# Two h tiles ahead of the second half of x, and the first w_in cast on one engine, in the first batch of an attention and MLP kernel

## Chip, core, metric

One core of one Trainium2 chip. The metric is device time in microseconds (us) per execution. Kernels that are compared ran in the same rounds on the same chip.

## The reference

Linear attention over 8 batches of 8 heads, 576 positions of 64 dimensions, then an MLP with an exact Gelu, in fp32:

```python
q_s = softmax(q, axis=-1)                 # per position
k_s = softmax(k, axis=2)                  # over positions
kv  = einsum('bhsd,bhse->bhde', k_s, v)
x   = einsum('bhsd,bhde->bhse', q_s, kv)  # -> [4608, 512]
h   = x @ w_in                            # w_in [512, 2048]
g   = 0.5 * h * (1 + erf(h / sqrt(2)))
out = g @ w_out                           # w_out [2048, 512]
```

(The softmaxes are written out in the reference; they are shortened here.)

## The kernel before

Matmuls run in bf16. Heads go in four pairs (hp 0 to 3): pairs 0 and 1 are "half 0", 2 and 3 "half 1". For each batch TensorE does kv, then x from normalised kv (kvc) and transposed q (qT); x is copied from PSUM, the memory into which TensorE writes, to xT in SBUF, from which it reads, one copy per pair; and h tile t (128 of the 2048 columns of h) sums over four dm, the blocks of 128 columns of x, where dm reads xT of pair dm:

```python
    def h_mm(c, ps, t, dms):
        for dm in dms:
            nc.tensor.matmul(
                ps, wi_bf[:, dm, t * 128:(t + 1) * 128], st[c]["xT"][:, dm, :],
                start=(dm == 0), stop=(dm == NDM - 1),
            )
```

In the traces each engine takes its instructions in the order of the program. Batch 0 is the one with little else to do: weights are still arriving. Its part, in the old order:

```python
    kv_mm(0, 0)
    kv_norm(0, 0)                # kvc of half 0: reciprocal and multiply, once per pair
    tp_mm(0, 1)
    tp_evac(0, 1)
    x_tile(0, 2, psum_a, "a")
    x_mm(0, 0)
    x_evac(0, 0, "s")            # "s": ScalarE; else VectorE
    cast_wi_dm(0, wi[0], 0, nc.scalar)
    for dm in range(1, NDM):
        cast_wi_dm(0, wi[0], dm, nc.gpsimd)
    kv_mm(0, 1)
    kv_norm(0, 1)                # kvc of half 1: both pairs at once
    x_evac(0, 1)
    x_tile(0, 3, psum_h, "h")
    x_mm(0, 1)
    x_evac(0, 2, "s")
    x_evac(0, 3)
    cast_wi(1, wi[1], "p")       # second w_in piece (tiles 2, 3), GpSimd
    table(AF.Gelu)
    ...
    h_phase(0, {0: [lambda: cast_wi(2, wi[2], "v")], ...}, groups={0: 2, 4: 4, 8: 4}, ...)
```

`wi[0]` is the first w_in piece, columns 0 to 255, that is h tiles 0 and 1; it is loaded in one transfer and cast to bf16 by dm.

The softmax here doesn't subtract the row's maximum and nothing guards it: scores larger than these inputs give would overflow.

Of the kernel before, what the change touches and what calls it, by code (L numbers as in the profile page):

```python
# [8 lines left out]
FP32 = mybir.dt.float32  # L9
# [7 lines left out]
def kernel(  # L17
# [16 lines left out]
    nc = tc.nc  # L34
# [4 lines left out]
    M = 128 * J  # L39
    R = S - M  # L40
    HP = H // 2
    NDM = DM // 128
# [10 lines left out]
    psum_h = ctx.enter_context(tc.tile_pool(name="psum_h", bufs=3, space=bass.MemoryType.PSUM))  # L53
    psum_y = ctx.enter_context(tc.tile_pool(name="psum_y", bufs=2, space=bass.MemoryType.PSUM))
    psum_a = ctx.enter_context(tc.tile_pool(name="psum_a", bufs=1, space=bass.MemoryType.PSUM))
# [12 lines left out]
    kvc = [singles.tile([128, HP, D], BF16, name=f"kvc{b}") for b in range(B)]  # L68
# [9 lines left out]
    def table(func):  # L78
        nc.scalar.activation(out=scr[:, 1:2], in_=scr[:, 0:1], func=func)  # L79

    st = [dict() for _ in range(B + 1)]
# [83 lines left out]
        for hp in range(HP):  # L165
            cast_v(b, hp)

    def kv_tiles(b):


        if b == 0:
            p = [psum_h.tile([128, 512], FP32, tag="h", name="kv")[:, 0:256] for i in range(2)]
            ps = psum_a.tile([128, 4, 256], FP32, tag="a2", name="kv")
            st[b]["kvall"] = ps[:, 0::2]
            p += [ps[:, 0, :], ps[:, 2, :]]
        else:
            ps = psum_a.tile([128, 4, 256], FP32, tag="a2", name="kv")
            st[b]["kvall"] = ps
            p = [ps[:, i, :] for i in place]
        st[b]["kv"] = p  # L180

    place = [1, 2, 0, 3]

# [4 lines left out]
    def kv_mm(b, half):  # L188


        if "kv" not in st[b]:
            kv_tiles(b)
        for n in range(NS):
            for i in range(2):
                for hh in range(2):
                    hp = 2 * half + i
                    pr = slice(hh * 64, hh * 64 + 64)
                    c = slice((hh ^ i) * 64, (hh ^ i) * 64 + 64)
                    nc.tensor.matmul(  # L199
                        st[b]["kv"][hp][c, 0:D + 1], ek[b % 2][pr, hp, n, :],  # L200
                        v_aug[b % 2][pr, hp, n, 0:D + 1], start=(n == 0), stop=(n == NS - 1),
                    )

    def kv_norm(b, half=None):

        ps = st[b]["kvall"]
        if half is None:
            parts = [(ps, kvc[b], 4)]
        elif b == 0 and half == 0:
            parts = [(st[b]["kv"][hp].unsqueeze(1), kvc[b][:, hp:hp + 1], 1) for hp in range(2)]  # L210
        elif b == 0:
            parts = [(ps, kvc[b][:, 2:4], 2)]
        else:
            parts = [(ps[:, 1:3] if half == 0 else ps[:, 0::3], kvc[b][:, 2 * half:2 * half + 2], 2)]
        for src, dst, m in parts:
            rec = small.tile([128, 4], FP32, tag="reck")
            nc.vector.reciprocal(rec[:, 0:m], src[:, :, D])
            nc.vector.tensor_tensor(  # L218
                out=dst, in0=src[:, :, 0:D],
                in1=rec[:, 0:m].unsqueeze(2).to_broadcast([128, m, D]), op=ALU.mult,  # L220
            )
# [39 lines left out]
    def tp_evac(b, half, eng="v"):  # L261
        o = st[b]["qT"][:, :, 2 * half:2 * half + 2, :]
        if eng == "v":
            nc.vector.tensor_copy(out=o, in_=st[b][f"tp{half}"])
        else:
            nc.scalar.copy(out=o, in_=st[b][f"tp{half}"])
# [12 lines left out]
    def x_tile(b, hp, pool, tag):  # L279
        if "xT" not in st[b]:  # L280
            st[b]["xT"] = attn_sb.tile([128, HP, M], BF16, tag="xT", name="xT")
        st[b][f"x{hp}"] = pool.tile([128, M], FP32, tag=tag, name="ps")

    def x_mm(b, half):

        for bb in range(B if b == B else 1):
            for r in range(2):
                for i in range(2):
                    hp = 2 * half + i
                    pr = slice(r * 64, r * 64 + 64)  # L290
                    c = slice((r ^ i) * 64, (r ^ i) * 64 + 64)
                    ps = st[b][f"x{hp}"]
                    if b < B:
                        nc.tensor.matmul(  # L294
                            ps[c, :], kvc_of(b, hp)[pr], st[b]["qT"][pr, :, hp, :],
                            start=True, stop=True,
                        )
                    else:
                        nc.tensor.matmul(  # L299
                            ps[c, bb * R:(bb + 1) * R], kvc_of(bb, hp)[pr],  # L300
                            st[b]["qT"][pr, bb // 2, hp, bb % 2 * R:(bb % 2 + 1) * R],
                            start=True, stop=True,
                        )

    def x_all(b):

        for hp in range(HP):
            pool, tag = (psum_h, "h") if hp < 3 else (psum_a, "a")
            x_tile(b, hp, pool, tag)
        x_mm(b, 0)  # L310
        x_mm(b, 1)
        for hp, eng in ((0, "s"), (2, "v"), (1, "s"), (3, "v")):
            x_evac(b, hp, eng)

    def x_evac(b, hp, eng="v"):
        ps = st[b][f"x{hp}"]
        if eng == "v":
            nc.vector.tensor_copy(out=st[b]["xT"][:, hp, :], in_=ps)  # L318
        else:
            nc.scalar.copy(out=st[b]["xT"][:, hp, :], in_=ps)  # L320

    def h_begin(c):
        st[c]["g"] = moe_sb.tile([128, NDF, M], BF16, tag="g", name="g", bufs=1)
# [8 lines that stand above are left out]
    def h_gelu(c, ps, t):  # L332
        nc.scalar.activation(out=st[c]["g"][:, t, :], in_=ps, func=AF.Gelu)  # L333
# [75 lines left out]
    def load_wi(i):  # L409

        w = wst.tile([128, NDM, 512], FP32, tag="w")
        n = wi_cols[i]
        src = moe_w_in[:, wi_off[i]:wi_off[i] + n].rearrange("(c p) f -> p c f", p=128)
        d = NDM // wi_parts[i]
        for c in range(0, NDM, d):
            nc.sync.dma_start(out=w[:, c:c + d, 0:n], in_=src[:, c:c + d])
        return w
# [3 lines left out]
    def cast_wi(i, w, eng):  # L421
        n = wi_cols[i]
        r = n // 128
        o = wi_bf[:, :, wi_off[i]:wi_off[i] + n].rearrange("p d (c m) -> p d c m", c=r)
        w = w[:, :, 0:n].rearrange("p d (m c) -> p d c m", c=r)
        if eng == "p":
            for h in range(2):
                nc.gpsimd.tensor_copy(out=o[:, 2 * h:2 * h + 2], in_=w[:, 2 * h:2 * h + 2])
        else:
            for c in range(NDM):  # L430
                nc.vector.tensor_copy(out=o[:, c], in_=w[:, c])  # L431

    def cast_wi_dm(i, w, dm, eng):

        n = wi_cols[i]
        r = n // 128
        o = wi_bf[:, dm, wi_off[i]:wi_off[i] + n].rearrange("p (c m) -> p c m", c=r)
        w = w[:, dm, 0:n].rearrange("p (m c) -> p c m", c=r)
        if eng is nc.scalar:
            eng.copy(out=o, in_=w)  # L440
        else:
            eng.tensor_copy(out=o, in_=w)

    def load_wo(i):
        w = wst.tile([128, 4, DM], FP32, tag="w")
# [19 lines left out]
    def cast_wo(i, w, c0=0, n=4, eng="v"):  # L465
        o, w = wo_bf[:, 4 * i + c0:4 * i + c0 + n, :], w[:, c0:c0 + n]
        if eng == "v":
            nc.vector.tensor_copy(out=o, in_=w)
        else:
            nc.scalar.copy(out=o, in_=w)  # L470
# [17 lines left out]
    wi = [load_wi(i) for i in range(5)]  # L488
# [28 lines left out]
    cast_v(0, 3, nc.gpsimd)  # L517
    x_tile(0, 0, psum_y, "y")
    x_tile(0, 1, psum_y, "y")
    kv_mm(0, 0)  # L520
    kv_norm(0, 0)
    tp_mm(0, 1)
    tp_evac(0, 1)
    x_tile(0, 2, psum_a, "a")
    x_mm(0, 0)
    x_evac(0, 0, "s")
    cast_wi_dm(0, wi[0], 0, nc.scalar)
    for dm in range(1, NDM):
        cast_wi_dm(0, wi[0], dm, nc.gpsimd)
    kv_mm(0, 1)  # L530
    kv_norm(0, 1)
    x_evac(0, 1)
    x_tile(0, 3, psum_h, "h")
    x_mm(0, 1)
    x_evac(0, 2, "s")
    x_evac(0, 3)
    cast_wi(1, wi[1], "p")
    table(AF.Gelu)

    def ybank():  # L540
        return psum_y.tile([128, M], FP32, tag="y", name="ps")
# [3 lines left out]
    def a2bank(i):  # L545
# [2 lines left out]
        return pair[0][:, i]  # L548

    h_phase(0, {  # L550
        0: [lambda: cast_wi(2, wi[2], "v")],
        2: [lambda: cast_wi(3, wi[3], "v")],
        6: [lambda: cast_wi(4, wi[4], "v")],
        9: [lambda: cast_wo(0, wo[0])],
        12: [lambda: cast_wo(1, wo[1])],
    }, groups={0: 2, 4: 4, 8: 4}, banks={
        3: ybank, 6: ybank, 8: ybank,
        9: lambda: psum_a.tile([128, M], FP32, tag="a", name="ps"),
        10: lambda: a2bank(0), 11: lambda: a2bank(1),
# [46 lines left out]
    hps = [psum_h.tile([128, M], FP32, tag="h", name="ps") for t in range(2)]  # L606
# [39 lines left out]
    for c in range(2, B + 1):  # L646
# [19 lines left out]
        if c < B:  # L666
            w = [lambda c=c: x_all(c + 1)]
# [34 lines left out]
```

## Time and profile before

| | before |
|---|---|
| time, median | 279.58 us (279.49 to 279.82, 3 runs); with the runs beside the change 279.53 (279.41 to 279.82, 6 runs) |
| TensorE busy | 97% of 278.0 us |
| granted TensorE clock | 1.00 |
| TensorE's wait for kvc of half 1 | 0.6 us, once |

The change touches four microseconds. TensorE in order of time (start, length, engine, line, operation, count; in brackets the idle time before and what ended it):

```profile
12.32 0.74 PE L294 MATMUL ps<-qT,kvc 64*64 64x512 bf16 x4
12.66 0.70 PE L199 MATMUL kv<-v_aug,ek 64*64 64x65 bf16 x36
13.98 0.41 PE L294 MATMUL ps<-qT,kvc 64*64 64x512 bf16 x4 [0.61 <-DVE kvc L218]
14.32 7.51 PE L327 MATMUL ps<-xT,wi_bf 128*128 128x512 bf16 x33
...
38.51 0.61 PE L255 MATMUL ps<-identity,e 128*128 128x128 bf16 x8
```

In order: x of half 0, kv of half 1, a hole of 0.61 us, x of half 1, then h without a break. The last line, the transposes of batch 1, serves as a milestone for how far TensorE has come.

### The profile page before, as it was taken

How to read it: one execution, taken by the hardware profiler on the slowest of the kernel's cores; microseconds unless marked ns; L12 is line 12 of the kernel's file. 1: busy time of each engine (PE TensorE's matmuls, PEld its weight loads, DVE VectorE, ACT ScalarE, POOL GpSimd, SP SyncE). 2: the span in 40 equal slices, each digit the busy share in tenths (PEclk: the TensorE clock that was granted, in tenths of full speed). 3: DMA queues.
4: the chain of work that ended last, by engine and by line, in shares of the span. 5: the costliest groups of instructions: out<-in, count | busy, mean ns of one | idle time of the engine just before them, and what ended most of it. 6: DMA issues, size and time to landing. Idle time of an engine off the chain costs nothing.

```text
span 278.0 us, 4534 instructions
## 1 busy us (share of the span) xinstructions
PE 270.0 (97%) x1891; PEld 126.5 (46%) x1919; DVE 100.7 (36%) x153; ACT 158.0 (57%) x247; POOL 32.8 (12%) x26
## 2 busy tenths in 40 slices
PE   7899999999999999999999999999999999999995
PEld 3444454444444444444444444444444444444443
DVE  2876574319743540093008400651015200130012
ACT  4867675789377816791569246943683363136400
POOL 1520051002020220014000500050005000000000
PEclk9999999999999999999999999999999999999999
DMA  7999999963993139702981199017502500220033
GB/s 253 398 386 429 397 402 407 398 257 103 287 348 61 66 79 295 283 38 86 267 329 40 42 247 383 38 51 190 115 0 75 151 2 0 75 78 0 0 78 77
DMA packets 44980, 50.10 MB, mean 180 GB/s; under 512 B 20384, under 2 KB 29856, under 8 KB 44704
## 3 DMA queue, kind: packets, MB, share of 16 engines
q1 hardware_dynamic: 44560, 49.39, 53.5%
q10 hardware_dynamic: 400, 0.43, 0.6%
q8 instruction: 15, 0.25, 0.3%
q14 instruction: 5, 0.04, 0.0%
HBM read 36.70 MB, written 9.44 MB: 166 GB/s over the span
## 4 chain that ended last, share of the span: by engine, by line
PE 94%; DMA 2%; issue 1%; ACT 1%; SPq 1%; DVE 0%
PE ps L327 44%; PE ps L355 43%; DMA f<-in_k_dram 2%; PE kv L199 2%; PE ps L294 2%; PE ps L380 1%; PE pair L327 1%; ACT ek L150 0%; ACT v_aug L160 0%; PE ps L255 0%; SPq L90 0%; PE ps L299 0%; SPq L103 0%; PE tp L255 0%; DVE kvc L218 0%
## 5 line engine op out<-in xcount | busy, mean ns | idle before, releaser
L327 PE MATMUL ps<-xT,wi_bf 128*128 128x512 bf16 x557 | 124.2, 380 | 0.5
L355 PE MATMUL ps<-wo_bf,g 128*128 128x512 bf16 x543 | 122.1, 380 | 1.6 <-issue 1.1
L333 ACT ACTIVATE g<-ps 128x512 bf16<-128x512 f32 x142 | 83.5, 598 | 66.8 <-PE ps L327 66.8
L327 PEld LDWEIGHTS <-wi_bf 128*128 128x128 bf16 x576 | 56.1, 98 | 68.0 <-issue 0.5
L355 PEld LDWEIGHTS <-g 128*128 128x128 bf16 x560 | 53.9, 98 | 64.3 <-issue 0.4
L363 DVE COPY y_sb<-ps 128x512 f32<-128x512 f32 x33 | 22.7, 687 | 81.7 <-PE ps L355 78.6
L238 POOL TENSOR_TENSOR e<-e,recq 128x2048 bf16<-128x2048 bf16 (+1 forms) x9 | 25.7, 2855 | 176.2 <-DVE recq L237 141.5
L162 DVE CAST v_aug<-f 128x576 bf16<-128x576 f32 x24 | 16.4, 746 | 47.5 <-DMA f<-in_v_dram 47.5
L236 DVE TENSOR_REDUCE qsum<-e 128x16 f32<-128x1024 bf16 (+1 forms) x13 | 21.1, 1621 | 14.4 <-ACT e L145 14.3
L320 ACT CAST xT<-ps 128x512 bf16<-128x512 f32 x18 | 9.9, 588 | 28.8 <-PE ps L294 18.8
L145 ACT ACTIVATE e<-f 128x512 bf16<-128x512 f32 (+1 forms) x42 | 20.5, 556 | 3.5 <-DMA f<-in_q_dram 3.5
L150 ACT ACTIVATE ek<-f 128x2304 bf16<-128x2304 f32 (+1 forms) x10 | 17.2, 1728 | 0.5 <-DMA f<-in_k_dram 0.4
L318 DVE CAST xT<-ps 128x512 bf16<-128x512 f32 x17 | 11.0, 686 | 17.0 <-PE ps L294 14.1
L79 ACT ACT_TABLE_LOAD x9 | 11.5, 1283 | 2.8 <-issue 2.6
L475 PE MATMUL ps<-zeros 128*128 128x512 f32 (+1 forms) x15 | 9.2, 773 | 1.5 <-DVE zeros L500 1.5
L145 ACT ACT_TABLE_LOAD x7 | 9.0, 1283 | 0.1
L431 DVE CAST wi_bf<-w 128x512 bf16<-128x512 f32 x12 | 7.3, 654 | 2.2 <-DMA w<-in_moe_w_in_dram 1.9
L199 PEld LDWEIGHTS <-ek 64*64 64x64 bf16 x576 | 6.6, 105 | 2.6 <-ACT wo_bf L470 0.4
L199 PE MATMUL kv<-v_aug,ek 64*64 64x65 bf16 x576 | 7.2, 194 | 0.2 <-ACT v_aug L160 0.2
L294 PE MATMUL ps<-qT,kvc 64*64 64x512 bf16 x62 | 5.7, 391 | 0.8 <-DVE kvc L218 0.6
L238 DVE TENSOR_TENSOR e<-e,recq 128x1024 bf16<-128x1024 bf16 x4 | 6.2, 1546 | 0.1
L475 PEld LDWEIGHTS ps<-zeros 128*128 128x128 f32 x14 | 3.5, 260 | 6.0 <-issue 4.5
(39 smaller groups left out, 49.9 us busy)
## 6 DMA issues: line engine op xcount, KB each, us to landing
out_dram<-y_sb SPq DMA_DIRECT2D x32, 256.0 KB, 2.4
f<-in_k_dram SPq DMA_DIRECT2D x6, 1152.0 KB, 9.7
f<-in_v_dram SPq DMA_DIRECT2D x6, 1152.0 KB, 11.7
f<-in_q_dram SPq DMA_DIRECT2D x6, 1024.0 KB, 7.2
w<-in_moe_w_in_dram SPq DMA_DIRECT2D x6, 512.0 KB, 8.7
f<-in_v_dram SPq DMA_DIRECT2D x8, 288.0 KB, 6.8
f<-in_q_dram SPq DMA_DIRECT2D x4, 512.0 KB, 12.5
w<-in_moe_w_out_dram SPq DMA_DIRECT2D x2, 1024.0 KB, 11.7
```

Source lines behind the costliest of these rows:

```text
L79: nc.scalar.activation(out=scr[:, 1:2], in_=scr[:, 0:1], func=func)
L145: nc.scalar.activation(out=dst[:, i], in_=src[:, u], func=AF.Exp)
L150: nc.scalar.activation(out=ek[b % 2][:, i:i + n], in_=st[b]["kf"][:, i:i + n].rearrange("p x (n d) -> p x n d", n=NS), func=AF.Exp,)
L162: eng.tensor_copy(out=o, in_=i)
L199: nc.tensor.matmul(st[b]["kv"][hp][c, 0:D + 1], ek[b % 2][pr, hp, n, :], v_aug[b % 2][pr, hp, n, 0:D + 1], start=(n == 0), stop=(n == NS - 1),
L236: nc.vector.reduce_sum(out=qsum, in_=eq[:, :, hs, :], axis=AX.X)
L238: eng.tensor_tensor(out=eq[:, :, hs, :], in0=eq[:, :, hs, :], in1=recq.unsqueeze(3).to_broadcast([128, J, w, D]), op=ALU.mult,)
L327: nc.tensor.matmul(ps, wi_bf[:, dm, t * 128:(t + 1) * 128], st[c]["xT"][:, dm, :], start=(dm == 0), stop=(dm == NDM - 1),)
L333: nc.scalar.activation(out=st[c]["g"][:, t, :], in_=ps, func=AF.Gelu)
L355: nc.tensor.matmul(ps, st[c]["g"][:, t, j * 128:(j + 1) * 128], wo_bf[:, t, :], start=(t == 0), stop=(t == NDF - 1),)
L363: nc.vector.tensor_copy(out=y_sb, in_=ps)
L475: nc.tensor.matmul(ps, z[:, 0:128], z, start=True, stop=True)
```

## The change

The intent is to fill the hole. dm 0 and 1 of h tiles 0 and 1 need only xT of pairs 0 and 1, so these four matmuls are put between kv of half 1 and x of half 1. For that, both copies of half 0 go to ScalarE, all four casts of the first w_in piece to GpSimd, and kv of half 0 into the two-bank PSUM tile (one reciprocal and one multiply for both pairs) while half 1 takes two single banks (two of each). The copies of half 1 change places: pair 2 goes to VectorE, pair 3 to ScalarE. The core of the diff, with cuts marked:

```diff
-        if b == 0:
+        if b == 0 and half == 1:
             p = [psum_h.tile([128, 512], FP32, tag="h", name="kv")[:, 0:256] for i in range(2)]
-            ps = psum_a.tile([128, 4, 256], FP32, tag="a2", name="kv")
-            st[b]["kvall"] = ps[:, 0::2]
-            p += [ps[:, 0, :], ps[:, 2, :]]
+            st[b]["kv"] += p
...
     x_mm(0, 0)
     x_evac(0, 0, "s")
-    cast_wi_dm(0, wi[0], 0, nc.scalar)
-    for dm in range(1, NDM):
+    x_evac(0, 1, "s")
+    for dm in range(NDM):
         cast_wi_dm(0, wi[0], dm, nc.gpsimd)
     kv_mm(0, 1)
     kv_norm(0, 1)
-    x_evac(0, 1)
+    h_begin(0)
+    hps = [psum_h.tile([128, M], FP32, tag="h", name="ps"),
+           psum_a.tile([128, 2, M], FP32, tag="a2", name="ps")[:, 0]]
+    for dm in (0, 1):
+        for t in range(2):
+            h_mm(0, hps[t], t, (dm,))
     x_tile(0, 3, psum_h, "h")
     x_mm(0, 1)
-    x_evac(0, 2, "s")
-    x_evac(0, 3)
+    x_evac(0, 2)
+    x_evac(0, 3, "s")
     cast_wi(1, wi[1], "p")
     table(AF.Gelu)
+    for dm in (2, 3):
+        for t in range(2):
+            h_mm(0, hps[t], t, (dm,))
+    for t in range(2):
+        h_gelu(0, hps[t], t)
+    cast_wi(2, wi[2], "v")
...
-    }, groups={0: 2, 4: 4, 8: 4}, banks={
+    }, t1=2, groups={4: 4, 8: 4}, banks={
```

More of the change, by code (lines that the diff above doesn't have):

```diff
@@ L166, in cast_v_all, with kv_tiles @@
             cast_v(b, hp)
-    def kv_tiles(b):
-        if b == 0:
+    def kv_tiles(b, half):
+        if b == 0 and half == 1:
             p = [psum_h.tile([128, 512], FP32, tag="h", name="kv")[:, 0:256] for i in range(2)]
-            ps = psum_a.tile([128, 4, 256], FP32, tag="a2", name="kv")
-            st[b]["kvall"] = ps[:, 0::2]
-            p += [ps[:, 0, :], ps[:, 2, :]]
-        else:
+            st[b]["kv"] += p
+        elif "kv" not in st[b]:
             ps = psum_a.tile([128, 4, 256], FP32, tag="a2", name="kv")
             st[b]["kvall"] = ps
-            p = [ps[:, i, :] for i in place]
-        st[b]["kv"] = p
+            st[b]["kv"] = [ps[:, 0, :], ps[:, 2, :]] if b == 0 else [ps[:, i, :] for i in place]
     place = [1, 2, 0, 3]
@@ L188, in kv_mm @@
     def kv_mm(b, half):
-        if "kv" not in st[b]:
-            kv_tiles(b)
+        kv_tiles(b, half)
         for n in range(NS):
@@ L208, in kv_norm @@
             parts = [(ps, kvc[b], 4)]
-        elif b == 0 and half == 0:
-            parts = [(st[b]["kv"][hp].unsqueeze(1), kvc[b][:, hp:hp + 1], 1) for hp in range(2)]
+        elif b == 0 and half == 1:
+            parts = [(st[b]["kv"][hp].unsqueeze(1), kvc[b][:, hp:hp + 1], 1) for hp in (2, 3)]
         elif b == 0:
-            parts = [(ps, kvc[b][:, 2:4], 2)]
+            parts = [(ps[:, 0::2], kvc[b][:, 0:2], 2)]
         else:
@@ L438, in cast_wi_dm @@
         w = w[:, dm, 0:n].rearrange("p (m c) -> p c m", c=r)
-        if eng is nc.scalar:
-            eng.copy(out=o, in_=w)
-        else:
-            eng.tensor_copy(out=o, in_=w)
+        eng.tensor_copy(out=o, in_=w)
     def load_wo(i):
@@ L519 @@
     x_tile(0, 1, psum_y, "y")
+    x_tile(0, 2, psum_a, "a")
     kv_mm(0, 0)
@@ L523 @@
     tp_evac(0, 1)
-    x_tile(0, 2, psum_a, "a")
     x_mm(0, 0)
     x_evac(0, 0, "s")
-    cast_wi_dm(0, wi[0], 0, nc.scalar)
-    for dm in range(1, NDM):
+    x_evac(0, 1, "s")
+    for dm in range(NDM):
         cast_wi_dm(0, wi[0], dm, nc.gpsimd)
@@ L550 @@
     h_phase(0, {
-        0: [lambda: cast_wi(2, wi[2], "v")],
         2: [lambda: cast_wi(3, wi[3], "v")],
```

## The prediction

> **What bounds the kernel now.** I read the page's busy shares first, then the waits of TensorE, then the pieces of the chain that ended last between 11 and 29 us, and last the time-ordered records of each engine from 10 to 20 us. The page and the list of TensorE's waits:
>
> ```profile
> PE 270.0 (97%) x1891; PEld 126.5 (46%) x1919; DVE 100.7 (36%) x153; ACT 158.0 (57%) x247; POOL 32.8 (12%) x26
> PE ps L475 <- DVE zeros L500: 1.5, 1, 1.5
> PE ps L355 <- issue: 1.1, 7, 0.2
> PE ps L294 <- DVE kvc L218: 0.6, 1, 0.6
> PE kv L199 <- ACT v_aug L160: 0.2, 1, 0.2
> ```
>
> The first line is busy time per engine; the others are who waited for whom, total us, times, longest. TensorE is busy 97%, and after the start-up it waits once for another engine: 0.6 us for kvc of the second half of batch 0. That hole is the target. The chain (start, length, what):
>
> ```profile
> 12.88 0.53 PE kv L199 x31
> ...
> 13.43 0.18 DVE rec L217
> 13.61 0.02 issue
> 13.64 0.30 DVE kvc L218
> 13.94 0.04 issue
> 13.98 0.41 PE ps L294 x4
> 14.39 0.75 PE ps L327 x3
> 15.14 0.05 issue
> 15.20 6.64 PE ps L327 x30
> ...
> 28.31 8.42 PE ps L355 x39
> ```
>
> From 13.98 on it is TensorE almost alone. So TensorE sets the time, and a microsecond won or lost at 14 us should reach the end nearly whole: no later wait on its list would absorb it. The other engines at this place (start, length, engine, line, operation, count, idle before and its releaser):
>
> ```profile
> 13.10 0.59 ACT L320 CAST xT<-ps 128x512 bf16<-128x512 f32 x1 [0.91 <-PE ps L294]
> 14.44 0.58 ACT L320 CAST xT<-ps 128x512 bf16<-128x512 f32 x1 [0.44 <-PE ps L294]
> 15.04 1.28 ACT L79 ACT_TABLE_LOAD   x1
> 13.85 1.32 DVE L318 CAST xT<-ps 128x512 bf16<-128x512 f32 x2
> 13.31 1.12 POOL L442 CAST wi_bf<-w 128x256 bf16<-128x256 f32 x3 [0.75 <-DMA w<-in_moe_w_in_dram]
> 14.66 1.23 POOL L428 CAST wi_bf<-w 128x512 bf16<-128x512 f32 x2 [0.23 <-DMA w<-in_moe_w_in_dram]
> ```
>
> The reader should see two things. GpSimd's first w_in cast starts at 13.31 because the load lands then; nothing in the change makes that earlier. And in the old order the copies of x from PSUM to SBUF (0.59 us on ScalarE, 0.69 on VectorE) run beside the first h matmuls: xT of pair 1 is copied at 13.85, of pair 2 at 14.44, of pair 3 at about 14.5, each in time for the dm that reads it. Only the wait for kvc is exposed.
>
> **What the Trainium skill says.** (1) "TensorE: Matmul & The Clock Gate", section "Phases on the wall clock" under Part 2, puts the gap of back-to-back 512-column matmuls at some 216 ns; this trace agrees (39 in 8.42 us, 0.2159 each). I use 0.216. (2) "PSUM — Partial Sum Buffer", section "Engine vs sequencer instructions": matmuls start and complete in program order. So an h matmul that waits for xT holds up all behind it; every TensorE wait in this trace is of that kind. (3) "VectorE: DVE Perf Modes", the errata section, gives PSUM-to-SBUF costs of 120+FD cycles at 0.96 GHz and 172+FD at 1.2 GHz: an estimate of 658 and 570 ns for 512 columns. The trace has 686 and 588 ns, and I use those: this is the latency that a dependent matmul sees. (4) "ScalarE: Activation LUTs", "What ACT_TABLE_LOAD costs": 1283 ns plus a drain of about 1380. The 1283 is here (1.28); the drain is not: the load starts at 15.04 and the first Gelu at 16.44. It matters for when the first Gelus can run.
>
> **The change, part by part.**
>
> *Half 0 normalised in one go.* kv of half 0 moves to the two-bank tile, so a reciprocal and a multiply serve both pairs (0.17 and 0.29 us, as half 1 did) instead of four instructions. Before: reciprocal at 11.84, second kvc ready at 12.59, the remaining x matmuls of half 0 at 12.65. After: kvc ready at about 12.33, all four x matmuls at 12.37 (the transposes ahead of them issue until about then), x ready about 12.8. Gain 0.28 us for half 0. kv of half 1 also needs v_aug of pair 3, which GpSimd finishes at 12.57 (11.90 plus 0.67), so it starts about 12.63 rather than behind x at 12.88 and ends about 13.1 instead of 13.36. By itself this gain would be on the path.
>
> *First w_in tiles into the hole.* Four h matmuls (dm 0 and 1, two tiles), 4 x 0.216 = 0.86 us, now stand before x of half 1. They need xT of pairs 0 and 1, both now copied by ScalarE: 12.82 to 13.41, and to about 13.9 (consecutive copies start 0.48 apart). And they need w_in, cast on GpSimd alone: 13.31 to 13.72 for dm 0 (0.41 each, starts 0.36 apart), 14.07 for dm 1. So the first h matmul starts not at 13.1 but at about 13.77 (0.05 after the cast), and the four run without a stall until 14.63. About 0.67 us of idle stays in front of them: the kvc hole becomes a hole for w_in, and the 0.28 us is lost in it.
>
> *x of half 1 behind them.* kvc of half 1 is ready by 13.9, long before. The four x matmuls start at 14.63 instead of 13.98. In the old trace ScalarE began its copy 0.46 after their start: so the copies begin at 15.09; ScalarE's (pair 3) ends at 15.68, VectorE's (pair 2, 0.69) at 15.78.
>
> *A new exposed copy.* The next in TensorE's order is dm 2 of the two tiles, which reads xT of pair 2; nothing stands between. TensorE has issued x by 14.97 (0.34 in the old trace, 13.98 to 14.32) and waits until about 15.82: some 0.85 us. Then dm 2 and dm 3 take 4 x 0.216 and tile 2 starts at 15.82 + 0.86 = 16.68.
>
> *The old order, for comparison.* First h matmul at 14.32; single records show the fifth at 15.20 and then steps of 0.215, the ninth (tile 2) at 16.06. **Sum:** 16.68 - 16.06 = +0.62 us. Checked by idle time: about 0.67 + 0.85 against 0.61 is +0.91, less the 0.28 by which half 0 and kv are earlier: +0.63.
>
> *Off the path.* ScalarE loses a 0.42 us cast and VectorE an x copy. The Gelu table load moves from 15.04 to about 15.68, the first Gelu from 16.44 to about 17.1; PSUM buffers that tiles 4 to 7 take again come free from 17.7, and need to be free from 18.4 on (tile 7, the fourth of its group, at 19.0, for a buffer free at about 18.8). Close, but no wait. GpSimd's second w_in piece ends at about 16.0 instead of 15.9, for use at 16.68. VectorE begins wi[2] at 15.8 instead of 15.3, needed from 18.4. All DMA is already in the queue.
>
> **Rivals.** (a) *The gap filler works*: four matmuls fill a 0.6 us hole, so 0.3 to 0.6 us is won, time 279.0 to 279.3. For it: the hole exists and TensorE is the bound. Against it: the same trace dates the w_in landing at 13.31, only 0.1 us before the hole begins, and what hid the copies of pairs 2 and 3 is now used up in front of them. It would need the casts half a microsecond sooner. (b) *A wash*: the new exposed copy and the gain cancel, or slack later swallows the difference: 279.4 to 279.8. Against it: no TensorE wait follows that a delay could hide in. (c) *Something later goes wrong*: late Gelus hold up PSUM buffers for tiles 4 to 7, or GpSimd's casts slow down beside VectorE: 280.5 to 281. Margins of 0.2 to 0.7 us speak against it, but the one for tile 7 is thin. (d) My sum: 280.2.
>
> **Range and chances.** 279.58 + 0.62 = 280.2 us. The pieces of half 0 and the cast are uncertain by some 0.15 us each, the exposed copy by 0.1, the runs scatter by 0.3; so 279.7 to 280.7 for 8 in 10. Two per cent is 5.6 us, far more than all work that the change touches: within 2% at 0.98, and 0.01 on either side.
>
> **What would show it right or wrong.** In the changed trace: (1) TensorE's first h matmul at about 13.8, with idle time before it put down to GpSimd's wi_bf or ScalarE's xT; (2) x of half 1 at about 14.6, and no wait for kvc there; (3) a TensorE wait of 0.7 to 0.9 us for xT of pair 2 on VectorE, new; (4) tile 2 at about 16.7; (5) no new TensorE wait from 17 to 30 us, and the whole chain after it shifted by 0.6. I am wrong if h starts before 13.4, if GpSimd's single casts take much longer than 0.41 us so that dm 1 stalls too, if dm 2 finds xT ready, or if the shift of 0.6 us is gone by 30 us.

## The result

The changed kernel takes 280.31 us (280.20 to 280.46, 6 runs), the kernel before 279.53 us in the same rounds (279.41 to 279.82, 6 runs): ratio 1.0027, 95% interval 1.0014 to 1.0040. So the time is the same at 2%, and slower by about 0.75 us. A ratio here is over the runs of the same rounds; it can differ by some 0.0003 from the ratio of the medians or of the means.

TensorE of the changed kernel, the same columns:

```profile
12.48 0.41 PE L290 MATMUL ps<-qT,kvc 64*64 64x512 bf16 x4
12.72 0.51 PE L195 MATMUL kv<-v_aug,ek 64*64 64x65 bf16 x36
13.57 1.08 PE L323 MATMUL ps<-xT,wi_bf 128*128 128x512 bf16 x3 [0.34 <-ACT xT L316]
14.58 0.41 PE L290 MATMUL ps<-qT,kvc 64*64 64x512 bf16 x4
15.78 6.63 PE L323 MATMUL ps<-xT,wi_bf 128*128 128x512 bf16 x30 [0.79 <-POOL wi_bf L424]
...
39.08 0.61 PE L251 MATMUL ps<-identity,e 128*128 128x128 bf16 x8
```

(One of the four early h matmuls has no record; the line counts three.) The hole of 0.61 us is now 0.34, and a new one of 0.79 has opened behind x of half 1. That is 0.34 + 0.79 - 0.61 = 0.52 us more idle time, out of a shift of the milestone by 39.08 - 38.51 = 0.57. The shift is the same at 261 us: the last long run of y matmuls starts at 261.13 instead of 260.56. Nothing later took it up.

The 0.34 is not a gain of 0.27, though. TensorE starts h when the first cast of w_in and the first copy to xT are done (13.50 and 13.52 here), and a kv that ends late only makes the idle time in front of it shorter. GpSimd later (below) has the same program up to here: its kv ended 0.26 us sooner, its idle time in front of h was 0.61, and yet h began at 13.58 and the milestone came at 39.06.

What the other engines did meanwhile:

```profile
12.93 1.07 ACT L316 CAST xT<-ps 128x512 bf16<-128x512 f32 x2 [0.67 <-PE ps L290]
15.06 0.59 ACT L316 CAST xT<-ps 128x512 bf16<-128x512 f32 x1 [1.06 <-PE ps L290]
15.03 0.69 DVE L314 CAST xT<-ps 128x512 bf16<-128x512 f32 x1 [0.99 <-PE ps L290]
13.09 1.47 POOL L435 CAST wi_bf<-w 128x256 bf16<-128x256 f32 x4 [0.72 <-DMA w<-in_moe_w_in_dram]
14.51 1.22 POOL L424 CAST wi_bf<-w 128x512 bf16<-128x512 f32 x2
```

There is a puzzle in these lines. VectorE's copy of xT of pair 2 ends at 15.03 + 0.69 = 15.72. GpSimd's second w_in piece, which tiles 0 and 1 do not read, ends at 14.51 + 1.22 = 15.73. dm 2 starts at 15.78, and the profile puts the wait down to GpSimd. By the program the wait is for xT; by the label it is for the cast. The first experiments settle that.

### The profile page after: what moved, and what is told of

Its sections match the earlier page's. It is cut to its first block, busy times and chain, and to the rows that moved or that the text cites. A ratio compares the mean times of both kernels' runs of the same rounds, so it can differ in the third digit from the quotient of the medians.

```text
span 278.5 us, 4538 instructions
## 1 busy us (share of the span) xinstructions
PE 270.1 (97%) x1891; PEld 126.7 (45%) x1919; DVE 99.4 (36%) x152; ACT 158.1 (57%) x247; POOL 33.2 (12%) x27
## 4 chain that ended last, share of the span: by engine, by line
PE 92%; DMA 4%; POOL 1%; issue 1%; SPq 0%; DVE 0%
PE ps L323 44%; PE ps L351 43%; DMA w<-in_moe_w_in_dram 2%; DMA f<-in_q_dram 2%; PE kv L195 2%; PE ps L290 1%; PE ps L376 1%; PE pair L323 1%; POOL wi_bf L435 1%; POOL wi_bf L424 0%; PE ps L295 0%; SPq L90 0%; PE ps L251 0%; PE tp L251 0%; DVE y_sb L381 0%
## 5 line engine op out<-in xcount | busy, mean ns | idle before, releaser
L150 ACT ACTIVATE ek<-f 128x2304 bf16<-128x2304 f32 (+1 forms) x10 | 17.1, 1726 | 0.4 <-DMA f<-in_k_dram 0.4
L314 DVE CAST xT<-ps 128x512 bf16<-128x512 f32 x16 | 10.4, 687 | 17.8 <-PE ps L290 15.0
L79 ACT ACT_TABLE_LOAD x9 | 11.5, 1283 | 2.8 <-issue 2.7
L145 ACT ACT_TABLE_LOAD x7 | 9.0, 1283 | 0.1
L461 DVE CAST wo_bf<-w 128x2048 bf16<-128x2048 f32 (+1 forms) x4 | 4.4, 1090 | 3.8 <-DMA w<-in_moe_w_out_dram 3.8
```

Of the source, the lines that this page charges most:

```text
L79: nc.scalar.activation(out=scr[:, 1:2], in_=scr[:, 0:1], func=func)
L145: nc.scalar.activation(out=dst[:, i], in_=src[:, u], func=AF.Exp)
L150: nc.scalar.activation(out=ek[b % 2][:, i:i + n], in_=st[b]["kf"][:, i:i + n].rearrange("p x (n d) -> p x n d", n=NS), func=AF.Exp,)
```

## Experiments

Theory: four matmuls ahead of x of half 1 delay x, and with it the copies to xT, which the old order hid behind those very four matmuls; the new wait is for xT of pair 2. Rival 1: the wait is for GpSimd's second w_in piece. Rival 2: the loss lies in the PSUM placement, in the casts, or in later Gelus.

"Mark" is the time in the trace from the first reciprocal of batch 0 to the first transposes of batch 1. It leaves out most of the scatter of the start; where w_in is what TensorE waits for (the change and the kernels with its order, and one h matmul ahead), the scatter of that load is still in it (27.39 against 27.15 for GpSimd later and the change). "Over before" is the difference of the mean times in the same rounds.

| kernel | median us | over before, us | ratio, 95% interval | mark us |
|---|---|---|---|---|
| before | 279.53 | | | 26.67 |
| the change | 280.31 | +0.75 | 1.0027 (1.0014 to 1.0040) | 27.15 |
| GpSimd later | 280.33 | +0.66 | 1.0023 (1.0011 to 1.0036) | 27.39 |
| pair 2 copied last | 280.92 | +1.20 | 1.0042 (1.0029 to 1.0056) | 27.91 |
| tiles 2, 3 in the hole | 279.85 | +0.23 | 1.0008 (0.9995 to 1.0020) | 27.04 |
| x between dm 0 and dm 1 | 279.92 | +0.21 | 1.0007 (0.9995 to 1.0020) | 26.92 |
| order only | 280.42 | +0.77 | 1.0029 (1.0017 to 1.0042) | 27.41 |
| placement only | 279.69 | +0.02 | 1.0003 (0.9990 to 1.0015) | 26.66 |
| casts only | 279.62 | -0.10 | 0.9995 (0.9983 to 1.0008) | 26.67 |
| one kv tile | 279.59; 279.67 | -0.09; -0.05 | 0.9999; 0.9997 | 26.42; 26.41 |
| one h matmul ahead | 279.65 | -0.04 | 1.0000 (0.9987 to 1.0014) | 26.63 |
| the same, two loads | 279.30; 279.70 | -0.37; -0.02 | 0.9986; 1.0001 | 26.34; 26.34 |

Five runs each, except six for the change; the kernel before had 9 runs in each of these rounds, with medians from 279.56 to 279.74. All outputs were correct.

### GpSimd's second piece later

```diff
+    nc.gpsimd.tensor_copy(out=pool_scr, in_=zeros32)   # useless work
     cast_wi(1, wi[1], "p")
```

> The changed kernel with one useless GpSimd copy (128x512, about 0.6 us) between the casts of the first and the second w_in piece, so that the second piece ends at about 16.3 us instead of 15.7. Theory (TensorE's new wait before dm 2 is for the copy of xT of pair 2 on VectorE, which ends at the same moment as the cast): dm 2 still starts at about 15.8, time 280.3 as the changed kernel. Rival (TensorE waits for the second w_in piece, as the trace of the changed kernel labels it): dm 2 starts at about 16.4 and the time grows by 0.6 to about 280.9.

Time as the changed kernel, and dm 2 starts at 15.75, while GpSimd finishes the second piece at 15.10 + 1.22 = 16.32:

```profile
13.58 1.04 PE L324 MATMUL ps<-xT,wi_bf 128*128 128x512 bf16 x4 [0.61 <-POOL wi_bf L436]
15.00 0.69 DVE L315 CAST xT<-ps 128x512 bf16<-128x512 f32 x1 [1.23 <-PE ps L291]
15.75 2.54 PE L324 MATMUL ps<-xT,wi_bf 128*128 128x512 bf16 x11 [0.79 <-POOL wi_bf L425]
15.10 1.22 POOL L425 CAST wi_bf<-w 128x512 bf16<-128x512 f32 x2
```

So TensorE does not wait for the piece to end, and xT of pair 2 was ready at 15.69. The label says GpSimd again, because now the first of the piece's two casts happens to end at 15.73. That first cast cannot be the releaser either: in the changed kernel it ended 0.6 us before dm 2 started. The label names whichever ended last.

### Pair 2 copied last

```diff
-    x_evac(0, 2)
-    x_evac(0, 3, "s")
+    x_evac(0, 3)
+    x_evac(0, 2)
```

> The changed kernel with both copies of half 1 on VectorE, pair 3 ahead of pair 2, so that xT of pair 2 is ready about 0.62 us later (about 16.35). Theory (xT of pair 2 releases dm 2): the wait before dm 2 grows from 0.8 to 1.4 us, dm 2 starts at about 16.4, time about 280.9. Rival (the GpSimd cast of the second piece releases it, and xT only happens to end then): dm 2 stays at 15.8 or is freed by whichever ends last, no clean shift by 0.62, time 280.3.

```profile
PE ps L323 <- DVE xT L314: 1.4, 1, 1.4
...
15.07 1.29 DVE L314 CAST xT<-ps 128x512 bf16<-128x512 f32 x2 [1.15 <-PE ps L290]
16.41 1.89 PE L323 MATMUL ps<-xT,wi_bf 128*128 128x512 bf16 x8 [1.39 <-DVE xT L314]
```

The second of VectorE's two copies, now that of pair 2, ends at 16.36. The wait grew from 0.79 to 1.39 us, and the median is 0.59 above that of GpSimd later, which ran in the same rounds with the wait of 0.79: as the theory had it. The later copy of pair 2 is paid in full.

### x between dm 0 and dm 1

```diff
-    for dm in (0, 1):
-        for t in range(2):
-            h_mm(0, hps[t], t, (dm,))
+    for t in range(2):
+        h_mm(0, hps[t], t, (0,))
     x_tile(0, 3, psum_h, "h")
     x_mm(0, 1)
+    for t in range(2):
+        h_mm(0, hps[t], t, (1,))
```

> The changed kernel with x of half 1 moved between dm 0 and dm 1 of the first two tiles. Theory: x starts at about 14.05, as kvc becomes ready, its copies start at about 14.5, xT of pair 2 is ready at about 15.2; dm 1 covers 0.43 us of the copy; the wait before dm 2 falls from 0.8 to about 0.4 us and the time by 0.5 to about 279.8. Rival (dm 2 waits for the GpSimd cast of the second piece, which this does not move): dm 2 stays at 15.8 and the time at 280.3.

```profile
14.49 0.69 DVE L314 CAST xT<-ps 128x512 bf16<-128x512 f32 x1 [0.76 <-PE ps L290]
15.24 2.97 PE L323 MATMUL ps<-xT,wi_bf 128*128 128x512 bf16 x13 [0.25 <-DVE xT L314]
14.46 1.23 POOL L424 CAST wi_bf<-w 128x512 bf16<-128x512 f32 x2
```

dm 2 now starts 0.45 us before GpSimd's second piece is done (15.69), behind xT of pair 2 (15.18). Rival 1 is out. Two of the four matmuls moved back behind x give back about 0.5 us of the 0.75; the wait left is 0.25, less than the 0.4 expected.

### Tiles 2 and 3 in the hole

dm 0 and 1 of tiles 2 and 3 go between x of half 1 and dm 2 of tiles 0 and 1 (the two further PSUM tiles are taken there, and the next cast moves up by a few lines of program):

```diff
+    hps += [psum_h.tile([128, M], FP32, tag="h", name="ps"),
+            psum_y.tile([128, M], FP32, tag="y", name="ps")]
+    for dm in (0, 1):
+        for t in (2, 3):
+            h_mm(0, hps[t], t, (dm,))
...
```

> The changed kernel with dm 0 and dm 1 of tiles 2 and 3 (four matmuls, 0.86 us) put between x of half 1 and dm 2 of tiles 0 and 1. Theory (the loss is the exposed latency of the copy, so other work in the hole removes it): the hole of 0.8 us shrinks to the 0.25 us until the first half of the second w_in piece is cast (15.15), dm 2 no longer waits, time about 279.7, 0.6 less than the changed kernel. Rival (the loss is elsewhere, in late Gelus or PSUM buffers): the time stays at 280.3 or rises.

```profile
14.90 0.41 PE L290 MATMUL ps<-qT,kvc 64*64 64x512 bf16 x4
15.58 2.76 PE L323 MATMUL ps<-xT,wi_bf 128*128 128x512 bf16 x12 [0.27 <-POOL wi_bf L424]
```

The hole is 0.27 us, here really held by the second w_in piece that these tiles do read, and there is no wait for xT behind it. About 0.5 us comes back (the trace is of the slowest of the five runs, 280.28 us, with a late start). The copy costs nothing when other work stands beside it.

In these five kernels, and in order only (below), the idle time can be added up: that in front of the first h matmul plus that in front of the matmuls behind x, less the 0.61 of the kernel before.

| kernel | idle, us | less 0.61 | over before, us |
|---|---|---|---|
| the change | 0.34 + 0.79 | +0.52 | +0.75 |
| GpSimd later | 0.61 + 0.79 | +0.79 | +0.66 |
| pair 2 copied last | 0.53 + 1.39 | +1.31 | +1.20 |
| tiles 2, 3 in the hole | 0.60 + 0.27 | +0.26 | +0.23 |
| x between dm 0 and dm 1 | 0.58 + 0.25 | +0.22 | +0.21 |
| order only | 0.34 + 0.79 | +0.52 | +0.77 |

So the usual idle time in front of h is near 0.6 us, as long as the old hole: next to nothing was filled. The two traces with 0.34 are those whose kv ends late against the landing of w_in (at 13.23 and 13.29 us, where GpSimd later has 12.97); there the sum falls short of the time, since it does not count when kv ends. In the other four, h starts 0.05 or 0.06 us after the end of GpSimd's first cast of w_in; where their labels name VectorE's kvc or reciprocal, which h does not read, that is again something that ended at the same moment.

### The parts by themselves

The new order and casts with the old kv placement (tile 2's bank then comes from the two-bank tile):

```diff
-    hps = [psum_h.tile(...), psum_a.tile([128, 2, M], FP32, tag="a2", name="ps")[:, 0]]
+    hps = [psum_h.tile([128, M], FP32, tag="h", name="ps") for t in range(2)]
```

> The changed order and casts with the kv placement of before. Theory (the order makes the loss, not the placement): h starts at about 13.75, x of half 1 at about 14.65, the wait before dm 2 is again 0.8 us, time 280.2 to 280.4, 0.6 to 0.8 over the kernel before. Rival (half 1 normalised in four instructions makes a good part of the loss): time at most 279.9.

```profile
15.85 1.67 PE L327 MATMUL ps<-xT,wi_bf 128*128 128x512 bf16 x7 [0.79 <-DVE xT L318]
```

The whole loss, +0.77 us, with the same wait of 0.79; in this trace the cast ended at 15.71 and the copy at 15.79, and the label is xT.

The kernel before with the new placement only (the `kv_tiles`, `kv_mm` and `kv_norm` hunks of the diff):

> The kernel before with only the kv placement of the changed kernel (half 0 in the two-bank tile, one reciprocal and one multiply; half 1 in two single banks, two of each). Theory (the placement moves the saving from half 1 to half 0 and back, so it is worth next to nothing): x of half 0 about 0.15 us earlier, kv of half 1 held by v_aug and ending about 0.1 us earlier, its kvc about 0.25 us longer in the making; x of half 1 starts about 0.1 us later than before, time 279.6 to 279.8. Rival (the placement is a real gain that the new order hides): time 0.15 to 0.3 us below the kernel before.

279.69 against 279.62 us, mark 26.66 against 26.67: nothing. What half 0 gains, half 1 gives back.

The kernel before with all casts on GpSimd:

```diff
-    cast_wi_dm(0, wi[0], 0, nc.scalar)
-    for dm in range(1, NDM):
+    for dm in range(NDM):
```

> The kernel before with only the casts of the changed kernel: all four of the first w_in piece on GpSimd, in the old order of TensorE. Theory (in the old order the casts have slack): dm 0 is cast by about 13.5 to 13.7 and dm 3 by 14.6 to 14.8, ahead of their matmuls at 14.3 and 15.6; no new wait, time 279.6, as before. Rival (GpSimd alone is too slow): a wait for wi_bf of 0.2 us or more, time 279.8 or above.

279.62 against 279.56 us, mark 26.67, no wait for wi_bf. The casts cost nothing in the old order; in the new order they were not varied alone, but the wait of 0.79 us is not for them (the first and third experiments). And the changed trace has no new TensorE wait from 17 to 30 us that late Gelus could have caused. So rival 2 is out, and the order makes the loss. One small share was not run by itself: the change of engines for half 1. ScalarE ended pair 3 at 15.06 + 0.59 = 15.65, so had it copied pair 2, as before, the wait would be shorter by an estimated 0.07 us.

### Can the hole be used at all?

First a shorter path through kvc: kv of all four pairs in one two-bank tile, so that each half takes one reciprocal and one multiply.

```diff
+        ps = psum_a.tile([128, 4, 256], FP32, tag="a2", name="kv")
+        st[b]["kvall"] = ps
+        st[b]["kv"] = [ps[:, i, :] for i in ((0, 2, 1, 3) if b == 0 else place)]
...
+            parts = [(ps[:, half::2], kvc[b][:, 2 * half:2 * half + 2], 2)]
```

> The kernel before, with kv of all four pairs of batch 0 in one two-bank tile (half 0 in columns 0 and 2, half 1 in 1 and 3), so that both halves take one reciprocal and one multiply. Nothing else moves. Theory (the path through kvc of half 1 is what TensorE waits for, so shortening it pays nearly in full): x of half 1 starts 0.15 us earlier against the start of kv, time about 279.45, 0.1 to 0.2 below the kernel before. Rival (the path is held by the w_in casts or by v_aug instead): no gain, 279.6.

> The one-tile kernel a second time, since its first five runs (279.59 against 279.62) did not show the 0.2 us that its trace showed as far as the end of the first batch. If the gain is real, 279.3 to 279.5 against 279.6; if the trace only caught a favourable start, 279.6 again.

x of half 1 starts 1.89 us after the first reciprocal in both traces, against 2.14 before, and both marks are 0.25 us shorter. The times do not show it: -0.09 and -0.05 us, with intervals of 0.3 us or more on either side. My expectation of 0.1 to 0.2 us was not met in time.

Then one h matmul instead of four ahead of x, on top of that (all casts on GpSimd, both copies of half 0 on ScalarE, that of pair 2 too):

```diff
     kv_norm(0, 1)
...
+    h_mm(0, hps[0], 0, (0,))
...
     x_mm(0, 1)
...
+    h_mm(0, hps[1], 1, (0,))
...
```

> The one-tile version with a single h matmul (dm 0 of tile 0) ahead of x of half 1, all casts of the first piece on GpSimd. Theory (work ahead of x pays only as far as it fits in the wait for kvc, since what comes after it delays the copies): the first w_in cast ends at 13.5 to 13.7, the matmul starts at 13.55 to 13.75 and ends about as kvc is ready (13.8), x starts at 13.8 to 14.0, xT of pair 2 (on ScalarE) is ready at 14.9 to 15.1, TensorE waits for it at most 0.2 us; time 279.3 to 279.5. Rival (any h matmul ahead of x loses, because the w_in landing is later than kvc): time above that of the one-tile version by 0.1 or more.

```profile
13.51 0.39 PE L316 MATMUL ps<-xT,wi_bf 128*128 128x512 bf16 x1 [0.61 <-POOL wi_bf L431]
13.83 0.41 PE L283 MATMUL ps<-qT,kvc 64*64 64x512 bf16 x4
```

No loss, and no gain: 279.65 us, where 279.3 to 279.5 was expected. There is no wait for xT any more, but the matmul waits 0.61 us, as long as the hole itself, for the w_in that has just been cast, and the mark is 0.2 us longer than that of one kv tile alone. So the load is split, that dm 0 and 1 land first (`wi_parts = [2, 1, 4, 2, 2]` in place of `[1, 1, 4, 2, 2]`):

> The version with one h matmul ahead, with the load of the first w_in piece in two halves (dm 0 and 1, then 2 and 3), so that dm 0 lands about 0.6 us sooner. Theory (what holds the first h matmul at 13.5 is the landing and cast of w_in): the first cast starts at about 12.4 to 12.6, behind v_aug on GpSimd, the matmul starts 0.2 to 0.3 us sooner, behind the copy of xT of pair 0, and x of half 1 follows as soon as kvc is ready, 1.9 us after the first reciprocal; time 0.1 to 0.3 below the kernel before. Rival (one more transfer delays the other loads and so kv): no gain, 279.6 or above.

> The version with one h matmul ahead and two loads a second time, to see whether 279.30 against 279.56 repeats. If it is real, 279.1 to 279.4, again 0.2 to 0.4 below the kernel before of the same rounds; if it was a favourable draw, 279.5 to 279.7.

GpSimd's first cast starts at 12.55 and 12.63 instead of 13.05, TensorE's wait falls to 0.34 us, and the mark is 26.34 in both traces, 0.33 below the kernel before. The times were 279.30 against 279.56 us (ratio 0.9986, interval 0.9973 to 1.0000) and 279.70 against 279.74 (1.0001, 0.9987 to 1.0014). The first looked like a gain and did not repeat. It is not shown that this version beats the kernel before, though in both rounds it lies below the 280.31 us of the change, by more than the runs scatter.

## Why the prediction was right

*Where the time goes.* The predicted 280.2 us and +0.62 stand against 280.31 us and +0.75 on average, inside the range. The two profiled executions took 279.74 and 280.31 us, 0.57 apart, as the traces are. The residue of some 0.1 us is within the scatter of the runs and was not resolved further.

*The first h matmul.* Predicted at 13.77 us, found at 13.57, because the first w_in piece was cast from 13.09 instead of 13.31; with unchanged loads that start lay anywhere from 13.04 to 13.47 in twelve traces. Both reasons given for its start held at once: GpSimd's cast of dm 0 ended at 13.50 and ScalarE's copy of pair 0 at 13.52. The idle time in front of it was 0.34 us in this trace, not 0.67, but 0.53 to 0.61 in the first four experiments: over-sized by about 0.1 there. The prediction let x of half 0 start at 12.37 and kv end at about 13.1; they came at 12.48 and, by the record, 13.23. The step itself, that the hole for kvc becomes a hole for w_in, held.

*The four without a stall.* Nearly: dm 1 began at 14.05, 0.05 after the copy of pair 1 ended at 14.00. x of half 1 came at 14.58 (predicted 14.63), with no wait for kvc. But from the first h matmul to x it took 1.01 us instead of 0.86: that stall, and 0.31 us instead of 0.216 from the last of the four to x. This makes up for most of the 0.20 by which h was early; that the later times agree so closely is partly luck.

*The exposed copy.* Predicted as a wait of some 0.85 us for xT of pair 2 on VectorE; it was 0.79, and the three experiments that moved the copy, or the work beside it, moved the time with it (pair 2 copied last; x between dm 0 and dm 1; tiles 2, 3 in the hole). This step carried the prediction. Its expected label was wrong in the changed trace, by a coincidence of 0.01 us.

*Tile 2.* Predicted at 16.68 us, recorded at 16.64; before, 16.06.

*Half 0 and the casts off the path.* The prediction said that what half 0 gains is lost. It is, but the placement alone shows a second reason: half 1's own normalisation takes as much longer (from its first reciprocal to the end of kvc 0.77 us instead of 0.50; mark 26.66 against 26.67).

*Nothing later.* The first Gelu moved to 17.07 (predicted 17.1), the thin margin for tile 7 held, no new TensorE wait followed, and the shift reached the end whole. (One reading of the old trace was too wide: not every TensorE wait there is for another engine's work, since the list puts 1.1 us in seven waits down to issue.)

*Rivals.* The gap filler (a) failed for the reasons given: w_in came too late for a full fill, and the four matmuls had been the cover of the copies. The wash (b) and a later trouble (c) did not occur.

*Left open.* Why the marks shorter by 0.25 to 0.33 us of the last versions are hardly seen in the times. The gain is not lost later: from the transposes of batch 1 to the last long run of y matmuls it is 222.05 us in the kernel before and 222.04 to 222.07 in these traces. It lies in the start or in the scatter: the first reciprocal came at 11.84 us before and at 11.68 to 11.99 in these. The intervals are wide enough to contain most of such a gain; no set of times shows it.

## What to carry to other kernels

Before filling an engine's hole with work from behind it, ask what that work was hiding: matmuls moved ahead of a producer no longer cover the copy of that producer's result, and the wait comes back behind it, here as 0.79 us for a hole that stayed open, because w_in was not there yet. Fill a hole only as far as the work is ready in it and ends when the awaited result arrives (here that lost nothing, and a gain is not shown), or bring other independent work into the place that was emptied (which gave back 0.5 us). And where two candidates end within a few hundredths of a microsecond of each other, don't trust the label of a wait: move one of them and look again.

## What the Trainium skill lacked or had wrong

- "TensorE: Matmul & The Clock Gate", section "Back-to-back issue gap": it gives about 131 ns per matmul as the sustained rate of a stream of 512-column matmuls with their weight loads. Here such streams ran at 216 ns each (39 in 8.42 us), which is the figure that the page calls the isolated gap.
- "ScalarE: Activation LUTs", section "What ACT_TABLE_LOAD costs": a drain of about 1380 ns beside the 1283 ns load. In the changed kernel the load starts at 15.67 us, and the next activation at 16.96: 1.29 us, with no such drain.
- None of the pages drawn on here says how much the landing of the first loads moves from one execution to the next: the first cast of w_in started at 13.04 to 13.47 us in twelve traces with the same loads, not much less than the effects studied.
